# Dense layer in blocks of 512 and 256 tokens instead of 384, and the small steps of ranks and places moved between the slices of the first expert

## The chip, the cores and the metric

The kernel runs on one core of a Trainium2 chip. The core has a matrix engine (PE; its weight loads are listed as PEld), a vector engine (DVE), a scalar engine (ACT), GpSimd (POOL) and a sync engine (SP) that here only issues DMAs. Each engine works through its own instructions in program order and waits on semaphores for the others. The metric is the device time of one execution in microseconds (us), the median of several runs. Runs of this kernel spread over about 0.14%.

## The reference, cut to what matters

Three stages are computed one after another: windowed attention, a mixture of eight experts of which each token takes one, and a dense two-layer block.

```python
# attention: B=4, H=8, S=576, D=64, window 128  ->  x of 2304 tokens x 512
# experts: E=8, 512 -> 1024 -> 512
expert_idx = np.argmax(logits, axis=1)
gate_w = probs[np.arange(N), expert_idx]
for e in range(E):
    mask = expert_idx == e
    h = np.maximum(x[mask] @ w1[e], 0.0)
    out[mask] = gate_w[mask, None] * (h @ w2[e])
# dense layer: 512 -> 2048 -> 512, w_in and w_out are given as float64
h = x @ w_in
g = np.where(h >= 1, h, np.where(h <= -1, 0.0, (h + 1) ** 2 / 4))
return g @ w_out
```

## The kernel before

Attention and routing fill the first 180 us. Their order is chosen at build time by a small planner (`drive`), which places steps by assumed costs. After it the program is written out by hand in plain order.

**Experts.** Experts are taken by rank, that is, by how many tokens chose them. Each is done in eight slices `ff` of 128 hidden units. A slice has 12 matmuls into a PSUM tile `bh` (tokens x first weights, three products of high and low parts: `xh`, `xl`, `whi`, `wlo`), then ACT makes `hh` (L1463) and DVE makes `hl` (L1464, the low part), and 12 matmuls into `by` (L1447 to L1449) use `hh` and `hl` one slice later: PE runs the 12 of slice ff+1 before the second 12 of slice ff. Between slices stand, on ACT and DVE, the splitting of raw weights into `whi` (L555) and `wlo` (L560), from slice 2 the tokens of the next expert (`xh`, `xl`), and from expert 1 on a generator `side`: sorting of token numbers, then the conversion of dense weights.

**Ranks and places.** Before the first expert's first `hl`, DVE reorders the table of gates by rank (`by_rank(gtable, gtable)`, L328 and L330) and works out where each expert's tokens start (`starts`, L1172 to L1193). `erank_i` from it is read by SP for the loads of later experts' weights.

**Dense weights.** `conv64` turns float64 weights of one 128-unit chunk into high and low float32 parts: for each of the two matrices DVE runs L1059, L1061, L1064 and the low part (`wc_0l`, `wc_1l`, L1052), and ACT runs L1043 (`cvr`) and L1067 (the high part). `NEARLY = 5` chunks are converted among the experts, the other 11 in the dense layer, from its third `in_part` on.

**Dense layer.** The 2304 tokens lie in six blocks of 384. `RUNS` takes blocks 0 and 1 together, 2 and 3 together, then 4, then 5. For each of 16 chunks `ff` of a block, `in_part` has 12 matmuls (L1539 to L1541) into one of two PSUM tiles `ch`; then ACT (`r`, L1545), DVE (L1547, L1549, the last to read `ch`), ACT (`gh`, L1550) and DVE (`gl`, L1553) form the activation. `out_part` runs, one chunk later (two in the last runs), three matmuls (L1565 to L1567) for each 128 tokens into one of six PSUM tiles `o`. At a block's end `put` copies each tile out (ACT L1579, DVE L1581 by turns) and POOL scatters it to the output (L1584). The input of a block is loaded by `load_y` and split by `split_y` (L1133, L1134).

Of the kernel before, what the change touches and what calls it, by code (L numbers as in the profile page):

```python
# [20 lines left out]
P = 128  # L21
# [10 lines left out]
CAPS = (384, 376, 344, 314, 296, 286, 274, 256)  # L32
L2, L3 = 2, 4
NRAW, NW, LEAD = 6, 7, 5
NEARLY = 5
BIAS = {"V": 1.2}
CONV = ((0, 0.0, 0.0), (1, 0.9, 1.5), (2, 3.0, 3.0), (3, 4.5, 4.5))
PEN = (0.03, 0.0, 0.8)
# [7 lines left out]
KEY = 4096  # L46
EVAC_DVE = (1, 3, 5, 7)
CT = CAP // P
GT, HT = 768, 384
QF = S - S % P  # L50
NSLOT = E * CT
NQ = NP * NT
# [4 lines left out]
def f(ap):  # L57
    return ap.bitcast(F32)
# [3 lines left out]
def fused_kernel(ctx, tc, qk, vT, v, emb, tau, w1, w2, win64, wout64, out):  # L62
# [956 lines left out]
    permu = const.tile([P, NQ], U32, name="permu")  # L1019
    pce = pool(ctx, "pce", 1)  # L1020
    pcv = pool(ctx, "pcv", 1)
    py = pool(ctx, "py", 3)
    wch = {}

    raw64 = {}
# [93 lines left out]
                nc.vector.tensor_scalar(at, at, float(P), None, op0=ALU.add)  # L1119
                nc.vector.tensor_scalar(rel_, rel_, -float(P), None, op0=ALU.add)  # L1120

    yt = {}

    def load_y(i):
        yl = py.tile([P, 4, CAP], F32R, tag="xl", name="yl")
        yh = py.tile([P, 4, CAP], F32R, tag="xh", name="yh")
        nc.sync.dma_start(f(yl), ysT[:, i * HT:(i + 1) * HT].rearrange("(c p) s -> p c s", p=P))
        yt[i] = (yh, yl)

    def split_y(i):  # L1130
# [6 lines left out]
    with ExitStack() as bb:  # L1137
# [122 lines left out]
        def order():  # L1260
            yield ask({"G": 2.1}, after=["rows"] + of_tiles("out", 0, NQ))
            gather(0)
            seen["gathered"] = end[0] + 2.5
            yield ask({"V": 0.66}, after=["ranked"], late=LATE[4])
            with nc.allow_low_precision(reason="whole numbers, of which one is not zero"):
                by_rank(tabu, table)
            yield ask({"G": 3.2}, end[0] + 0.13)
            gather(1)
            yield ask({"V": 0.66}, after=[("gates", NP - 1)], late=LATE[4])
            by_rank(gtable, gtable)  # L1270

        def ranks_and_starts():
            yield vec(0.1, ["count"], late=LATE[4])
            for _ in rank_experts():
                yield vec(0.15, late=LATE[4])
            seen["ranked"] = end[0] + 0.13
            yield vec(0.15, late=LATE[4])
            for _ in starts():
                yield vec(0.15, late=LATE[4])

        def new_xT():
            xh = py.tile([P, 4, CAP], F32R, tag="xh", name="xh")
            xl = py.tile([P, 4, CAP], F32R, tag="xl", name="xl")
# [136 lines left out]
        for e in range(E):  # L1420
# [31 lines left out]
            for ff in range(8):  # L1452
# [59 lines left out]

    pcl = pool(ctx, "pcl", 1)
    pg = pool(ctx, "pg", 3)
    po = pool(ctx, "po", 2)
    ps_h = pool(ctx, "ps_ch", 2, space=PSUM)
    ps_o = pool(ctx, "ps_co", 1, space=PSUM)
    gap = const.tile([1, 1], F32, name="gap")
    halfc = const.tile([P, 1], F32, name="halfc")
    nc.gpsimd.memset(halfc, 0.5)  # L1520
    cv = conv64(range(NEARLY, FF // P), pcl)
    TH = HT // P

    RUNS = (((0, 1), 0, 1), ((2, 3), 0, 1), ((4,), 0, 2), ((5,), TH, 2))
    outs, parts = {}, [0]

    def more():

# [3 lines left out]
    def in_part(hf, ff):  # L1532
        parts[0] += 1
        w1h, w1l = wch[ff][:2]
        yh, yl = yt[hf]
        hp = ps_h.tile([P, HT], F32, tag="ch", name="ch")
        for c in range(4):
            o = slice(c * P, (c + 1) * P)
            nc.tensor.matmul(hp, w1h[:, o], yh[:, c], start=(c == 0), stop=False)  # L1539
            nc.tensor.matmul(hp, w1h[:, o], yl[:, c], start=False, stop=False)  # L1540
            nc.tensor.matmul(hp, w1l[:, o], yh[:, c], start=False, stop=(c == 3))  # L1541
        r = pg.tile([P, HT], F32, tag="r", name="r", bufs=2)
        a = pg.tile([P, HT], F32R, tag="gh", name="gh", bufs=4)
        b = pg.tile([P, HT], F32R, tag="gl", name="gl", bufs=4)
        nc.scalar.activation(r, hp, AF.Relu, bias=halfc, scale=0.5)  # L1545
        more()
        nc.vector.scalar_tensor_tensor(r, r, 1.0, r, op0=ALU.min, op1=ALU.mult)  # L1547
# [7 lines left out]
        return a, b  # L1555

    def out_tile(run, ff, gs, i, t):
        halves, b0, _ = run
        _, _, w2h, w2l = wch[ff]
        hf = halves[i]  # L1560
        gh, gl = gs[i]
        if ff == 0:
            outs[hf, t] = ps_o.tile([P, DM], F32, tag=f"o{b0 + i * TH + t}", name=f"o{b0 + i * TH + t}")
        o, out_ = slice(t * P, (t + 1) * P), outs[hf, t]
        nc.tensor.matmul(out_, gh[:, o], w2h, start=(ff == 0), stop=False)  # L1565
        nc.tensor.matmul(out_, gl[:, o], w2h, start=False, stop=False)  # L1566
        nc.tensor.matmul(out_, gh[:, o], w2l, start=False, stop=(ff == FF // P - 1))  # L1567
        if ff == FF // P - 1:
            put(hf, t)

    def out_part(run, ff, gs):
        for i in range(len(gs)):
            for t in range(TH):
                out_tile(run, ff, gs, i, t)

    def put(hf, t):
        ot = po.tile([P, DM], F32, tag="ot", name="ot", bufs=3)
        if t % 2 == 0:
            nc.scalar.activation(ot, outs.pop((hf, t)), AF.Copy)  # L1579
        else:  # L1580
            nc.vector.tensor_copy(ot, outs.pop((hf, t)))  # L1581
        k = hf * TH + t
# [5 lines left out]

    todo, coming = [], iter(())
    for run in RUNS:  # L1590
        halves, _, lag = run
        ahead = [h for h in (halves[0] + 2, halves[0] + 3) if len(halves) == 2 and h < N // HT]
        if ahead:
            load_y(ahead[0])
            coming = split_y(ahead[0])
        for ff in range(FF // P):
            gs = []
            for hf in halves:
                gs.append(in_part(hf, ff))
                if ahead and ff == FF // P - 1 and hf == halves[0]:  # L1600
                    del yt[hf]
                    load_y(ahead[1])
# [56 lines left out]
```

## Time and profile before

| | |
|---|---|
| time before, median of 3 runs | 822.54 us (822.37 to 823.5) |
| the profiled execution's own time | 822.19 us |
| its span, first to last instruction | 820.5 us |
| PE busy | 806.9 us (98%) |
| DVE busy | 516.9 us (63%) |
| ACT busy | 421.5 us (51%) |
| POOL busy | 137.7 us (17%) |
| mean DMA rate | 129 GB/s |
| granted TensorE clock, mean | 0.999 |

PE is busy nearly all the time, so the question for each stage is whether it ever waits, and how long one matmul takes from its start to the start of the next. The busy time of a matmul row overlaps the next one's, since matmuls are pipelined; distances between starts are what counts. The span is 1.69 us shorter than the execution's own time.

### The profile page before, as it was taken

To read this page: it belongs to the slowest core of one execution; us is meant where nothing else is said; L and a number is where in the kernel's file an instruction comes from. 1 tells how busy PE (TensorE), PEld (TensorE's weight loads), DVE (VectorE), ACT (ScalarE), POOL (GpSimd) and SP (SyncE) were. 2 spreads that over 40 slices of the span, in tenths; PEclk is the share of its full clock that TensorE was granted. 3 is DMA by queue.
4 is the path that set the end of the run, shared out by engine and by line. 5 is a ranking of instruction groups with operands and counts; after the bars stand their busy time and mean duration, and the time that the engine had idled before them with its cause. 6 is when DMAs were issued, how large, how long until landed. Compare 5 with 4: busy or idle time off the path is not lost.

```text
span 820.5 us, 14256 instructions
## 1 busy us (share of the span) xinstructions
PE 806.9 (98%) x5242; PEld 749.8 (91%) x5242; DVE 516.9 (63%) x1390; ACT 421.5 (51%) x881; POOL 137.7 (17%) x205
## 2 busy tenths in 40 slices
PE   9999999999999999999999999999999999999996
PEld 7999999869999999999998989999999999999995
DVE  7777767897667687777469898544343454344332
ACT  7879899856435466566345555333222333223221
POOL 5975664031110110100000000011000003001001
PEclk9999999999999999999999999999999999999999
DMA  9846942648645668776134332021000012001001
GB/s 335 308 158 237 330 160 71 227 160 277 202 159 166 216 216 276 241 235 198 62 116 128 129 122 84 1 100 55 0 1 1 1 40 77 1 1 40 1 0 39
DMA packets 59180, 106.03 MB, mean 129 GB/s; under 512 B 3942, under 2 KB 35686, under 8 KB 59104
## 3 DMA queue, kind: packets, MB, share of 16 engines
q1 hardware_dynamic: 55776, 95.15, 34.7%
q0 software_dynamic: 3328, 9.90, 3.5%
q8 instruction: 43, 0.70, 0.3%
q14 instruction: 33, 0.27, 0.1%
HBM read 90.42 MB, written 14.62 MB: 128 GB/s over the span
## 4 chain that ended last, share of the span: by engine, by line
issue 56%; PE 12%; POOL 2%; ACT 0%; DVE 0%; POOLq 0%; ACTq 0%
PE bh L1458 2%; POOL out L1584 2%; PE bh L1460 2%; PE bh L1459 2%; PE by L1447 2%; PE by L1449 2%; PE by L1448 2%; PE bx L1295 1%; ACT whi L555 0%; DVE wlo L560 0%; POOL gap L1583 0%; PE permp L1385 0%; POOLq L1655 0%; POOL xg L1166 0%; ACT yo L1497 0%
## 5 line engine op out<-in xcount | busy, mean ns | idle before, releaser
L1547 DVE SCALAR_TENSOR_TENSOR r<-r 128x384 f32<-128x384 f32 x96 | 53.4, 556 | 120.6 <-ACT r L1545 117.1
L1539 PE MATMUL ch<-yh,wc_0h 128*128 128x384 f32 x384 | 129.2, 336 | 0.0
L1541 PE MATMUL ch<-yh,wc_0l 128*128 128x384 f32 x384 | 129.1, 336 | 0.0
L1540 PE MATMUL ch<-yl,wc_0h 128*128 128x384 f32 x384 | 128.7, 335 | 0.0
L1545 ACT ACTIVATE r<-ch,halfc 128x384 f32<-128x384 f32 x96 | 55.2, 575 | 117.4 <-PE ch L1541 117.1
L1550 ACT ACTIVATE gh<-r 128x384 fp32r<-128x384 f32 x96 | 50.5, 526 | 123.4 <-DVE r L1549 123.4
L1566 PE MATMUL o<-wc_1h,gl 128*128 128x512 f32 x288 | 113.3, 393 | 0.1
L1567 PE MATMUL o<-wc_1l,gh 128*128 128x512 f32 x288 | 113.3, 393 | 0.0
L1565 PE MATMUL o<-wc_1h,gh 128*128 128x512 f32 x288 | 112.0, 389 | 0.0
L1584 POOL DMA_INDIRECT out<-ot,permu x18 | 17.5, 973 | 462.2 <-ACT ot L1579 458.9
L560 DVE TENSOR_TENSOR wlo<-wraw,whi 128x1024 fp32r<-128x1024 f32 x64 | 78.0, 1222 | 20.1 <-ACT whi L555 19.6
L1553 DVE TENSOR_TENSOR gl<-r,gh 128x384 fp32r<-128x384 f32 x96 | 53.4, 557 | 43.7 <-ACT gh L1550 42.6
L1458 PE MATMUL bh<-xh,whi 128*128 128x256 f32 (+6 forms) x256 | 80.2, 313 | 0.0
L1448 PE MATMUL by<-hl,whi 128*128 128x256 f32 (+6 forms) x256 | 77.5, 303 | 1.8 <-DVE hl L1464 1.8
L1447 PE MATMUL by<-hh,whi 128*128 128x256 f32 (+6 forms) x256 | 77.3, 302 | 0.0
L1449 PE MATMUL by<-hh,wlo 128*128 128x256 f32 (+6 forms) x256 | 77.3, 302 | 0.0
L1460 PE MATMUL bh<-xh,wlo 128*128 128x256 f32 (+6 forms) x256 | 77.1, 301 | 0.0
L1459 PE MATMUL bh<-xl,whi 128*128 128x256 f32 (+6 forms) x256 | 76.9, 301 | 0.0
L1539 PEld LDWEIGHTS ch<-yh,wc_0h 128*128 128x128 f32 x384 | 72.1, 188 | 2.9 <-DVE r L1549 0.3
L1540 PEld LDWEIGHTS ch<-yl,wc_0h 128*128 128x128 f32 x384 | 72.1, 188 | 2.5
L1541 PEld LDWEIGHTS ch<-yh,wc_0l 128*128 128x128 f32 x384 | 72.0, 188 | 0.0
L555 ACT ACTIVATE whi<-wraw 128x1024 fp32r<-128x1024 f32 x64 | 67.3, 1055 | 0.7 <-ACTq L1476 0.7
(270 smaller groups left out, 1718.9 us busy)
## 6 DMA issues: line engine op xcount, KB each, us to landing
wraw<-in_w SPq DMA_DIRECT2D x64, 512.0 KB, 4.6
rqk<-in_qk SPq DMA_DIRECT2D x30, 576.0 KB, 5.1
raw<-in_w_in SPq DMA_DIRECT2D x16, 512.0 KB
raw<-in_w_out SPq DMA_DIRECT2D x16, 512.0 KB, 4.7
vT<-in_vT SPq DMA_DIRECT2D x16, 288.0 KB, 2.8
yl<-ysT SPq DMA_DIRECT2D x6, 768.0 KB, 6.0
x_dram<-xt SPq DMA_DIRECT2D x8, 512.0 KB, 6.6
vt<-in_v SPq DMA_DIRECT2D x8, 438.0 KB, 6.8
```

What stands on the lines that cost most here:

```text
L1447: nc.tensor.matmul(y, w2h[:, o], hh[:, :cap], start=(ff == 0), stop=False)
L1448: nc.tensor.matmul(y, w2h[:, o], hl[:, :cap], start=False, stop=False)
L1449: nc.tensor.matmul(y, w2l[:, o], hh[:, :cap], start=False, stop=(ff == 7))
L1458: nc.tensor.matmul(hp, w1h[:, o], xh[:, c, :cap], start=(c == 0), stop=False)
L1459: nc.tensor.matmul(hp, w1h[:, o], xl[:, c, :cap], start=False, stop=False)
L1460: nc.tensor.matmul(hp, w1l[:, o], xh[:, c, :cap], start=False, stop=(c == 3))
L1539: nc.tensor.matmul(hp, w1h[:, o], yh[:, c], start=(c == 0), stop=False)
L1540: nc.tensor.matmul(hp, w1h[:, o], yl[:, c], start=False, stop=False)
L1541: nc.tensor.matmul(hp, w1l[:, o], yh[:, c], start=False, stop=(c == 3))
L1565: nc.tensor.matmul(out_, gh[:, o], w2h, start=(ff == 0), stop=False)
L1566: nc.tensor.matmul(out_, gl[:, o], w2h, start=False, stop=False)
L1567: nc.tensor.matmul(out_, gh[:, o], w2l, start=False, stop=(ff == FF // P - 1))
```

## The change

- **Blocks.** The dense layer's tokens lie in blocks of 512, 256, 512, 512 and 512 (`SIZES`). The first run takes the blocks of 512 and 256 together, the others one block each. `in_part` writes a `ch` tile of up to 512 columns, two of them as before. Output tiles take the six PSUM tiles `o` in turn.
- **Buffers.** Expert tokens (`xh`, `xl`) move to a pool of two buffers of their own; the dense blocks have places of their own (`yl0`, `yl1`, `yl2`). `gh` and `gl` have two buffers of each width; those of the last block lie in the space of the fourth block's input, four deep. Output copies use the conversion's `cvr` and `cva` buffers, two each, in place of three `ot`.
- **Early chunks.** `NEARLY` goes from 5 to 3, so 13 chunks are converted in the dense layer.
- **Ranks and places.** Of `starts`, only the part up to `erank_i` stays ahead of the first expert. The rest, with the gate table put by rank, is called two steps at a time after each slice of expert 0 from slice 1 on.

```diff
-NEARLY = 5
+NEARLY = 3
...
-GT, HT = 768, 384
+SIZES = (512, 256, 512, 512, 512)
+GT = max(SIZES)
...
-    py = pool(ctx, "py", 3)
+    py = pool(ctx, "py", 1)
...
     def load_y(i):
-        yl = py.tile([P, 4, CAP], F32R, tag="xl", name="yl")
-        yh = py.tile([P, 4, CAP], F32R, tag="xh", name="yh")
-        nc.sync.dma_start(f(yl), ysT[:, i * HT:(i + 1) * HT].rearrange("(c p) s -> p c s", p=P))
+        t0, n = sum(SIZES[:i]), SIZES[i]
+
+        place, tag = ((py, 0), (py, 1), (late[0], 2), (py, 0), (late[0], 2))[i]
+        yl = place.tile([P, 4, n], F32R, tag=f"yl{tag}", name="yl")
+        yh = place.tile([P, 4, n], F32R, tag=f"yh{tag}", name="yh")
+        nc.sync.dma_start(f(yl), ysT[:, t0:t0 + n].rearrange("(c p) s -> p c s", p=P))
...
             nc.vector.tensor_copy(erank_i, erank)
             yield
+            by_rank(gtable, gtable)
+            yield
             pick(nc.vector, nov, cnt, True, tmp)
...
-            yield ask({"V": 0.66}, after=[("gates", NP - 1)], late=LATE[4])
-            by_rank(gtable, gtable)
...
-            yield vec(0.15, late=LATE[4])
-            for _ in starts():
-                yield vec(0.15, late=LATE[4])
...
         drive(lambda: streams)
+        places = starts()
+        next(places)
...
                 if e > 0:
                     for _ in range(3 if e < 3 else 2):
                         next(side, None)
+                elif ff > 0:
+
+                    for _ in range(2):
+                        next(places, None)
...
-    RUNS = (((0, 1), 0, 1), ((2, 3), 0, 1), ((4,), 0, 2), ((5,), TH, 2))
-    outs, parts = {}, [0]
+    RUNS = ((0, 1), (2,), (3,), (4,))
+    first_tile = [sum(SIZES[:i]) // P for i in range(len(SIZES))]
+    outs, parts, wide = {}, [0], []
...
-        hp = ps_h.tile([P, HT], F32, tag="ch", name="ch")
+        n = SIZES[hf]
+        hp = ps_h.tile([P, GT], F32, tag="ch", name="ch")[:, :n]
...
-        a = pg.tile([P, HT], F32R, tag="gh", name="gh", bufs=4)
-        b = pg.tile([P, HT], F32R, tag="gl", name="gl", bufs=4)
+        r = pg.tile([P, GT], F32, tag="r", name="r", bufs=2)[:, :n]
+        if hf == len(SIZES) - 1:
+
+            if ff == 0:
+                wide.extend(py.tile([P, 4, GT], F32R, tag=f"{t}0", name=f"{t}w") for t in ("yh", "yl"))
+            a, b = (w[:, ff % 4] for w in wide)
+        else:
+            a = pg.tile([P, n], F32R, tag=f"gh{n}", name="gh", bufs=2)
+            b = pg.tile([P, n], F32R, tag=f"gl{n}", name="gl", bufs=2)
...
+            bank = (first_tile[hf] + t) % 6
+            outs[hf, t] = ps_o.tile([P, DM], F32, tag=f"o{bank}", name=f"o{bank}")
...
-        ot = po.tile([P, DM], F32, tag="ot", name="ot", bufs=3)
+
+        ot = f(pcv.tile([P, 512], I32, tag=("cvr", "cva")[t % 2], name="ot", bufs=2))
...
-        halves, _, lag = run
-        ahead = [h for h in (halves[0] + 2, halves[0] + 3) if len(halves) == 2 and h < N // HT]
-        if ahead:
-            load_y(ahead[0])
-            coming = split_y(ahead[0])
+        halves, lag = run, 2 if run == RUNS[-1] else 1
+        if halves[-1] + 1 < len(SIZES):
+            load_y(halves[-1] + 1)
+            coming = split_y(halves[-1] + 1)
...
-    for n, t in ((0, 0), (1, 0), (0, 1), (1, 1), (0, 2), (1, 2)):
-        out_tile(*todo[n], 0, t)
+
+    for t in range(SIZES[-1] // P):
+        for step in todo:
+            out_tile(*step, 0, t)
```

Three places show how instructions move; all are on DVE. The line numbers of the changed kernel are larger than those of the kernel before by 2 to 15 for the same statement.

The first place is the start of expert 0. In the kernel before, the 20 steps of ranks and places stand between the last `xl` (low part of the tokens of expert 0) and the first `hl`; these are the last ten of them and what follows:

```order
L1181 CAST sti<-stf 128x8
L1182 TENSOR_TENSOR nov<-nov,caps 128x8
L1184 TENSOR_SCALAR nov<-nov 128x8
L1185 CAST novi<-nov 128x8
L1187 TENSOR_SCALAR novi<-novi 128x8
L1188 TENSOR_REDUCE anyo<-novi 128x1
L149 TENSOR_TENSOR tmp_2996<-rank1h,stf 128x64
L150 TENSOR_REDUCE ste<-tmp_2996 128x8
L1192 SCALAR_TENSOR_TENSOR kbase<-erank,caps 128x8
L1193 TENSOR_SCALAR toki<-tokhi,pid 128x18
L1464 SCALAR_TENSOR_TENSOR hl<-bh,hh 128x256
L560 TENSOR_TENSOR wlo<-wraw,whi 128x1024 x2
```

In the changed kernel, from that last `xl` on:

```order
L1292 TENSOR_TENSOR xl<-bx,xh 128x256 x4
L1177 MEMSET one_2986 128x8
L151 TENSOR_TENSOR tmp_2996<-rank1h,ranks 128x64
L152 TENSOR_REDUCE erank<-tmp_2996 128x8
L1179 CAST erank_i<-erank 128x8
L1468 SCALAR_TENSOR_TENSOR hl<-bh,hh 128x256
L562 TENSOR_TENSOR wlo<-wraw,whi 128x1024 x2
L1468 SCALAR_TENSOR_TENSOR hl<-bh,hh 128x256
L562 TENSOR_TENSOR wlo<-wraw,whi 128x1024
L330 TENSOR_TENSOR tm<-gtable,rank1h 128x192
L332 TENSOR_REDUCE gtable<-tm 128x24
L151 TENSOR_TENSOR tmp_2996<-rank1h,cnt 128x64
```

Four of the 20 steps are left ahead of the first `hl`; the other 16 stand in groups of four behind the slices 1 to 4.

The second place is the start of expert 6 (`hl` of 274 columns). Before, behind the copies `yo` of the last expert's result and a `wlo`, steps of the conversion (`cva`, `wc_1l`) stand ahead of the second and third `hl`:

```order
L560 TENSOR_TENSOR wlo<-wraw,whi 128x1024
L1061 SCALAR_TENSOR_TENSOR cva<-raw_7005,cva 128x512
L1064 ISA cva<-cva,cvr 128x1024
L1464 SCALAR_TENSOR_TENSOR hl<-bh,hh 128x274
L560 TENSOR_TENSOR wlo<-wraw,whi 128x1024
L1070 TENSOR_TENSOR wc_1l<-cva,wc_1h 128x512
L1464 SCALAR_TENSOR_TENSOR hl<-bh,hh 128x274
L560 TENSOR_TENSOR wlo<-wraw,whi 128x1024
L1134 TENSOR_TENSOR yl<-yl,yh 128x384
```

In the changed kernel:

```order
L562 TENSOR_TENSOR wlo<-wraw,whi 128x1024
L1468 SCALAR_TENSOR_TENSOR hl<-bh,hh 128x274
L562 TENSOR_TENSOR wlo<-wraw,whi 128x1024
L1468 SCALAR_TENSOR_TENSOR hl<-bh,hh 128x274
L562 TENSOR_TENSOR wlo<-wraw,whi 128x1024
L1139 TENSOR_TENSOR yl<-yl,yh 128x512
L1468 SCALAR_TENSOR_TENSOR hl<-bh,hh 128x274
```

The conversion steps are gone from here; they belong to the fifth chunk, which the change leaves to the dense layer.

The third place is the start of the dense layer, `r` and `gl` being the two results of the activation on DVE. Before:

```order
L1547 SCALAR_TENSOR_TENSOR r<-r 128x384
L1549 TENSOR_TENSOR r<-ch,r 128x384
L1553 TENSOR_TENSOR gl<-r,gh 128x384
L1547 SCALAR_TENSOR_TENSOR r<-r 128x384
L1549 TENSOR_TENSOR r<-ch,r 128x384
L1553 TENSOR_TENSOR gl<-r,gh 128x384
L1547 SCALAR_TENSOR_TENSOR r<-r 128x384
L1059 TENSOR_SCALAR cva<-raw_7108 128x512
```

In the changed kernel:

```order
L1562 SCALAR_TENSOR_TENSOR r<-r 128x512
L1564 TENSOR_TENSOR r<-ch,r 128x512
L1568 TENSOR_TENSOR gl<-r,gh 128x512
L1562 SCALAR_TENSOR_TENSOR r<-r 128x256
L1564 TENSOR_TENSOR r<-ch,r 128x256
L1568 TENSOR_TENSOR gl<-r,gh 128x256
L1562 SCALAR_TENSOR_TENSOR r<-r 128x512
L1061 TENSOR_SCALAR cva<-raw_6629 128x512
```

The passes are the same in number and order; the first `in_part` has passes of 512 columns and the second of 256, where both had 384.

## Rows read from the trace of the kernel before

**Rows 1.** PE by stage: window, length, busy (count), clock, DMA share, GB/s.

```profile
181.85:413.82 231.97, 229.33 (x1659) 1.00 0.62 200
413.82:684.01 270.19, 270.19 (x1370) 1.00 0.18 59
684.01:814.07 130.06, 129.98 (x649) 1.00 0.05 19
```

**Rows 2.** Waits of PE's weight loads over the whole span; total us, times, longest.

```profile
PEld by L1448 <- DVE hl L1464: 2.5, 3, 1.7
...
PEld o L1566 <- DVE gl L1553: 0.4, 1, 0.4
...
PEld ch L1539 <- DVE r L1549: 0.3, 2, 0.2
```

**Rows 3.** Timeline of PE, expert 0; columns: start, length, instruction, idle before.

```profile
185.55 0.28 PE L1447 MATMUL by<-hh,whi 128*128 128x256 f32 x1
187.37 0.39 PE L1448 MATMUL by<-hl,whi 128*128 128x256 f32 x1 [1.54 <-DVE hl L1464]
```

**Rows 4.** Timeline of ACT (first row) and DVE, expert 0.

```profile
183.95 0.38 ACT L1463 ACTIVATE hh<-bh 128x256 fp32r<-128x256 f32 x1 [0.89 <-PE bh L1460]
...
183.06 0.41 DVE L328 TENSOR_TENSOR tm<-gtable,rank1h 128x192 f32<-128x192 f32 x1
...
186.76 0.23 DVE L1193 TENSOR_SCALAR toki<-tokhi,pid 128x18 f32<-128x18 f32 x1
186.90 0.41 DVE L1464 SCALAR_TENSOR_TENSOR hl<-bh,hh 128x256 fp32r<-128x256 f32 x1
```

**Rows 5.** Timeline of PE (two rows) and DVE, start of expert 6.

```profile
370.90 0.29 PE L1447 MATMUL by<-hh,whi 128*128 128x274 f32 x1
...
371.65 0.29 PE L1449 MATMUL by<-hh,wlo 128*128 128x274 f32 x1
...
369.60 0.68 DVE L1061 SCALAR_TENSOR_TENSOR cva<-raw,cva 128x512 int32<-128x512 int32 x1
...
370.93 0.43 DVE L1464 SCALAR_TENSOR_TENSOR hl<-bh,hh 128x274 fp32r<-128x274 f32 x1
```

**Rows 6.** Timeline of PE: first matmuls of stretches, expert 0 and first dense run.

```profile
190.22 0.28 PE L1447 MATMUL by<-hh,whi 128*128 128x256 f32 x1
...
191.66 0.28 PE L1458 MATMUL bh<-xh,whi 128*128 128x256 f32 x1
...
447.30 0.39 PE L1565 MATMUL o<-wc_1h,gh 128*128 128x512 f32 x1
...
451.42 0.33 PE L1539 MATMUL ch<-yh,wc_0h 128*128 128x384 f32 x1
...
455.61 0.39 PE L1565 MATMUL o<-wc_1h,gh 128*128 128x512 f32 x1
```

**Rows 7.** Timelines at the start of the dense layer: ACT, DVE, PE.

```profile
416.16 0.58 ACT L1545 ACTIVATE r<-ch,halfc 128x384 f32<-128x384 f32 x1 [2.12 <-PE ch L1541]
...
417.37 0.56 DVE L1549 TENSOR_TENSOR r<-ch,r 128x384 f32<-128x384 f32 x1
...
417.98 0.44 PE L1539 MATMUL ch<-yh,wc_0h 128*128 128x384 f32 x1
```

**Rows 8.** Groups by line (three from 510 us): busy, mean ns, idle.

```profile
L1549 DVE TENSOR_TENSOR r<-ch,r 128x384 f32<-128x384 f32 x72 | 40.1, 557 | 2.5
...
L1579 ACT ACTIVATE ot<-o 128x512 f32<-128x512 f32 x12 | 6.8, 592 | 12.7 <-DMA out<-ot,permu 9.2 <-PE o L1567 3.6
L1581 DVE COPY ot<-o 128x512 f32<-128x512 f32 x6 | 4.1, 687 | 9.7 <-DMA out<-ot,permu 7.5 <-PE o L1567 2.2
...
L560 DVE TENSOR_TENSOR wlo<-wraw,whi 128x1024 fp32r<-128x1024 f32 x64 | 78.0, 1222 | 20.1 <-ACT whi L555 19.6
```

**Rows 9.** Timeline of ACT, two places of the first dense run.

```profile
445.48 0.58 ACT L1545 ACTIVATE r<-ch,halfc 128x384 f32<-128x384 f32 x1 [0.35 <-PE ch L1541]
...
469.25 0.67 ACT L1043 ACTIVATE cvr<-raw 128x512 int32<-128x512 uint32 x1 [0.63 <-DMA raw<-in_w_in]
```

More of the change, by code (lines that the diff above doesn't have):

```diff
@@ L1120, in overflow @@
                 nc.vector.tensor_scalar(rel_, rel_, -float(P), None, op0=ALU.add)
-    yt = {}
+    yt, late = {}, [None]
     def load_y(i):
-        yl = py.tile([P, 4, CAP], F32R, tag="xl", name="yl")
-        yh = py.tile([P, 4, CAP], F32R, tag="xh", name="yh")
-        nc.sync.dma_start(f(yl), ysT[:, i * HT:(i + 1) * HT].rearrange("(c p) s -> p c s", p=P))
+        t0, n = sum(SIZES[:i]), SIZES[i]
[3 more added lines that the diff above has]
+        nc.sync.dma_start(f(yl), ysT[:, t0:t0 + n].rearrange("(c p) s -> p c s", p=P))
         yt[i] = (yh, yl)
@@ L1276, in ranks_and_starts @@
             seen["ranked"] = end[0] + 0.13
-            yield vec(0.15, late=LATE[4])
-            for _ in starts():
-                yield vec(0.15, late=LATE[4])
         def new_xT():
-            xh = py.tile([P, 4, CAP], F32R, tag="xh", name="xh")
-            xl = py.tile([P, 4, CAP], F32R, tag="xl", name="xl")
+            xh = px.tile([P, 4, CAP], F32R, tag="xh", name="xh")
+            xl = px.tile([P, 4, CAP], F32R, tag="xl", name="xl")
             return xh, xl
@@ L1514, in fused_kernel @@
     pg = pool(ctx, "pg", 3)
-    po = pool(ctx, "po", 2)
+    late[0] = pool(ctx, "pz", 1)
     ps_h = pool(ctx, "ps_ch", 2, space=PSUM)
@@ L1521, in fused_kernel @@
     cv = conv64(range(NEARLY, FF // P), pcl)
-    TH = HT // P
-    RUNS = (((0, 1), 0, 1), ((2, 3), 0, 1), ((4,), 0, 2), ((5,), TH, 2))
-    outs, parts = {}, [0]
+    RUNS = ((0, 1), (2,), (3,), (4,))
+    first_tile = [sum(SIZES[:i]) // P for i in range(len(SIZES))]
+    outs, parts, wide = {}, [0], []
     def more():
@@ L1541, in in_part @@
             nc.tensor.matmul(hp, w1l[:, o], yh[:, c], start=False, stop=(c == 3))
-        r = pg.tile([P, HT], F32, tag="r", name="r", bufs=2)
-        a = pg.tile([P, HT], F32R, tag="gh", name="gh", bufs=4)
-        b = pg.tile([P, HT], F32R, tag="gl", name="gl", bufs=4)
+        r = pg.tile([P, GT], F32, tag="r", name="r", bufs=2)[:, :n]
[6 more added lines that the diff above has]
+            b = pg.tile([P, n], F32R, tag=f"gl{n}", name="gl", bufs=2)
         nc.scalar.activation(r, hp, AF.Relu, bias=halfc, scale=0.5)
@@ L1557, in out_tile @@
     def out_tile(run, ff, gs, i, t):
-        halves, b0, _ = run
+        halves = run
         _, _, w2h, w2l = wch[ff]
@@ L1562, in out_tile @@
         if ff == 0:
-            outs[hf, t] = ps_o.tile([P, DM], F32, tag=f"o{b0 + i * TH + t}", name=f"o{b0 + i * TH + t}")
+            bank = (first_tile[hf] + t) % 6
+            outs[hf, t] = ps_o.tile([P, DM], F32, tag=f"o{bank}", name=f"o{bank}")
         o, out_ = slice(t * P, (t + 1) * P), outs[hf, t]
@@ L1572, in out_part @@
         for i in range(len(gs)):
-            for t in range(TH):
+            for t in range(SIZES[run[i]] // P):
                 out_tile(run, ff, gs, i, t)
     def put(hf, t):
-        ot = po.tile([P, DM], F32, tag="ot", name="ot", bufs=3)
+        ot = f(pcv.tile([P, 512], I32, tag=("cvr", "cva")[t % 2], name="ot", bufs=2))
         if t % 2 == 0:
@@ L1581, in put @@
             nc.vector.tensor_copy(ot, outs.pop((hf, t)))
-        k = hf * TH + t
+        k = first_tile[hf] + t
         nc.gpsimd.memset(gap, 0.0)
@@ L1599, in fused_kernel @@
                 gs.append(in_part(hf, ff))
-                if ahead and ff == FF // P - 1 and hf == halves[0]:
-                    del yt[hf]
-                    load_y(ahead[1])
             todo.append((run, ff, gs))
@@ L1607, in fused_kernel @@
                 next(coming, None)
-        if ahead:
-            for _ in split_y(ahead[1]):
-                pass
-    for n, t in ((0, 0), (1, 0), (0, 1), (1, 1), (0, 2), (1, 2)):
-        out_tile(*todo[n], 0, t)
+    for t in range(SIZES[-1] // P):
+        for step in todo:
+            out_tile(*step, 0, t)
 _OUTS = [((2304, 512), "float32")]
```

## Prediction

> **What bounds the kernel now.** I read the stages first. From the first expert to the dense layer PE is busy 229.33 of 231.97 us, in the first two runs of the dense layer all of 270.19, in the last two 129.98 of 130.06, always at the granted clock 1.00, which is the upper of its two levels, 2.4 GHz [rows 1]. So from 181.85 us on the time is the number of matmuls times the distance between their starts, plus the few waits. Then the waits of PE's weight loads [rows 2]: the reader is to see that three lines matter to this change. The second product of a slice waits for `hl` three times, 2.5 us in all and 1.7 at the longest; the dense layer waits 0.3 us for the last reader of a `ch` tile, in two places, and 0.4 us once at its end for `gl`. DVE and ACT cost nothing where they are not in these lines. Third, the timeline at each of these places [rows 3 to 5, 7], and last, the starts of long stretches of matmuls, which give their true price [rows 6]: the row's own length overlaps the next.
>
> **The change part by part.** *Ranks and places.* In expert 0 PE starts the first matmul into `by` at 185.55 and the second at 187.37, 1.82 us later where 0.12 is usual [rows 3, 6]. It waits for `hl`, which DVE starts at 186.90. Its input `hh` was done at 183.95 + 0.38 = 184.33; but DVE worked from 183.06 on through the 20 small steps, the last at 186.76 [rows 4]. With four steps left ahead of it (the order of the changed kernel), the small steps end near 183.8, `hl` waits for `hh` and is done near 184.8, 0.9 before PE asks. That takes off 1.82 - 0.12 = 1.7 us. The other 16 steps are not free, they are about 0.2 us each, 0.8 behind each of slices 1 to 4. A slice of PE is 24 matmuls of 0.12, or 2.9 us; DVE's own work in it is one `wlo` of 1.22 [rows 8], one `hl` of 0.41 [rows 4] and, from slice 3, an `xl` of about 0.5: with 0.8 more, 2.5 to 2.9. Since `hl` is asked for a whole stretch of 12 matmuls after PE made its input (1.4 us), I take no new wait. Bounds of this term: 1.7 off, or, if a later `hl` comes as late as 1.2 us of one `wlo`, 0.5 off. Behind the moved steps wait the gate scaling of expert 1 on ACT (in slice 2, after the gate table, which comes in slice 1) and the store of expert 0 (in expert 1); neither is near. `erank_i`, for which SP waits before it loads the ninth raw weight, comes a little earlier.
>
> *Three early chunks instead of five.* In expert 6, two conversion steps stand ahead of `hl` on DVE: it starts L1061 at 369.60 and `hl` only at 370.93, and PE takes 0.75 us from 370.90 to 371.65 for two matmuls [rows 5]. The other short wait for `hl` is of the same kind. Both belong to chunks that the change leaves to the dense layer. What is left of the line is 2.5 - 1.7 = 0.8 us [rows 2], and I take all of it off. The cover is checked at the other end: the dense layer converts one chunk in each pair of `in_part`, as before, so a chunk is ready about a pair (8.3 us) ahead of its use rather than three; the rate is the same.
>
> *Blocks.* Run 1 before: 18 matmuls of 512 columns take 451.42 - 447.30 = 4.12 us, 0.2289 each; 24 of 384 take 455.61 - 451.42 = 4.19, 0.1746 each; 12 of 256, in expert 0, take 191.66 - 190.22 = 1.44, 0.120 each [rows 6]. Columns stay (2304 x 16 x 12), second-layer matmuls stay (18 tiles x 16 x 3 = 864). First-layer ones go from 6 x 16 x 12 = 1152 of 384 to 4 x 16 x 12 = 768 of 512 and 192 of 256: 1152 x 0.1746 = 201.1 us become 768 x 0.2289 + 192 x 0.120 = 198.8, so 2.3 off. The three prices lie on a line with about 11 ns per matmul whatever its columns, and 192 matmuls are saved. Bounds: nothing, if the price of a 512-column first-layer matmul is that of 384 by columns (0.2328), and 2.9, if all 15 ns beyond the columns at 2.4 GHz (0.2289 against 0.2133) belong to the matmul.
>
> The Trainium skill (TensorE: Matmul & The Clock Gate, section Back-to-back issue gap) gives an isolated gap of N / 2.4 + 2.5 ns, that is 2.5 ns per matmul where these rows show some 11. By it the blocks would save 192 x 2.5 ns = 0.5 us.
>
> *The first wait of the dense layer.* PE does the first chunk of both blocks and then wants the first `ch` tile back. Before, 24 matmuls x 0.1746 = 4.2 us after its start at 413.82 it had just been read: ACT starts at 416.16, DVE's last pass at 417.37 ends at 417.93, PE goes on at 417.98 [rows 7]. Now the same 4.2 us pass (12 x 0.2289 + 12 x 0.120), but the first block's 12 matmuls end later by 12 x 0.054 = 0.65, and its passes are longer: DVE 0.687 in place of 0.557 twice, a copy standing for the two, and ACT about 0.1 longer (0.58 at 384 [rows 7]; at 512 between 0.592, a plain copy, and 0.58 x 512 / 384 = 0.77) [rows 8]. The tile was free 417.93 - 413.82 = 4.11 after the start, and is now at 4.11 + 0.65 + 0.26 + 0.10 = 5.1: PE waits 0.9 to 1.0 instead of 0.2, 0.8 more (0.7 to 0.95). The second tile, of 256, is free in time.
>
> *The rest.* At the end, the last `gl` is later by three DVE passes and two of ACT, but out matmuls of four tiles rather than three cover it: 0.4 stays. The last copy is DVE's (0.687) instead of ACT's (0.592) [rows 8]: 0.1 more. Loads of inputs go out earlier than they are needed, into free places; more output buffers can only shorten waits that PE does not see. I take nothing for these.
>
> **Sum:** -1.7 - 0.8 - 2.3 + 0.8 + 0.1 = -3.9 us. The profiled execution takes 822.19, its span 820.5; the median of the runs is 822.54, 0.35 above. So span 816.6, own time 818.3, median 818.6.
>
> **The rivals.** *Price by column.* A larger matmul saves nothing, because what lies beyond the columns grows with them: 512 columns at 0.2328. For it: no row has a first-layer matmul of 512. Against it: 256, 384 and 512 lie on one line that does not pass through zero [rows 6]. Then 818.6 + 2.3 = 820.9. With the 2.5 ns per matmul of the Trainium skill (same page and section) it would be 820.4; the rows do not agree with that constant.
>
> *The stall in expert 0 moves.* The small steps meet `wlo` and `xl` in slices 2 to 4 where DVE is full; one late `hl` gives back up to 1.2: 819.8. Against it: 1.4 us of notice.
>
> *The converter chain of run 1 becomes the bound, and the kernel is slower.* ACT and DVE in turn serve the activation and a chunk's conversion; in a pair of `in_part` (8.3 us) ACT has only 0.35 us in which it waits for PE, so the chain takes 7.95 [rows 9]. Now 13 pairs convert instead of 11, the splits of the next input (four DVE passes of 0.687) fall on three pairs that also convert, and in a 512 part the raw load has less time between its issue and its use; one load already made ACT wait 0.63 [rows 9]. If every pair overruns by x, 13 x is lost, once the slack before PE misses the second `ch` tile (about 2 us, an estimate: half a pair, less the passes) has been used up by the three splits, 3 x 0.687 = 2.1. With the 0.63 wait in every pair, x = 0.63 - 0.35 = 0.28: 3.6 lost, 822.2, no change. It is slower by 0.2% (1.65 us) from x = (3.9 + 1.65) / 13 = 0.43 on; with two such waits per pair, x = 0.91, it gives 830.4. Against it: only two loads of the run show a wait at all, and DVE's columns per pair are the same (768).
>
> **How the numbers follow.** 0.2% is about what a measurement of this kernel can tell from no change. My forecast, 817.3 to 819.6 by the bounds of its terms, 0.62; price by column 0.13; moved stall 0.08; converter chain 0.11, of which 0.04 near 822 and 0.07 slower; any other loss or gain 0.06. Faster than 820.9: the forecast, the moved stall, half of price by column (0.06, since it ends on the line) and 0.02 of the rest, so 0.78; slower: 0.07 of the chain and 0.01 of the rest, so 0.08; within 0.2%: what is left, 0.14. The range 816.6 to 821.4 holds the forecast, the first two rivals and a margin for a larger saving; what is left out is the chain and half of the rest.
>
> **What the next profile shows.** Right: no wait of PE for `hl` in expert 0, 5 or 6; the dense layer starts near 411.3; 12 matmuls of 512 into `ch` in about 2.75 us and a pair of run 1 still near 8.3, a chunk of a single block at 5.5; one wait of about 1 us for the first `ch` tile. Wrong: a wait for `ch` repeated through run 1 (chain), a 512 matmul at 0.233 (price by column), a wait for `hl` in slices 2 to 4 of expert 0.

## Result and the profile after

The changed kernel takes 814.07 us (median of 4 runs, 813.93 to 814.38), the one before, measured beside it, 822.64. The ratio is 0.9892, interval 0.988 to 0.9904: 8.6 us less, where I had forecast 3.9 less and 816.6 as the lower end. The direction and the places were right; the size was not. The profiled execution takes 813.93 us, its span is 812.2, 8.3 shorter than before.

First the stages of the profile after (for the same statement its line numbers are 2 to 17 larger than before, not 2 to 15): experts, the first run of the dense layer, its other three runs. The columns are window, length, busy time and count of PE, PEld, DVE, ACT and POOL, then clock, DMA share and GB/s; they answer to [rows 1].

```profile
181.86:410.36 228.50, 227.93 (x1658) 223.35 (x1657) 153.60 (x295) 123.19 (x210) 20.16 (x21) 1.00 0.60 194
410.36:539.63 129.27, 128.41 (x656) 109.71 (x655) 110.19 (x205) 66.39 (x120) 0.00 (x0) 1.00 0.37 118
539.63:805.47 265.84, 265.60 (x1170) 219.25 (x1169) 109.27 (x160) 72.08 (x113) 17.06 (x33) 1.00 0.05 19
```

The experts take 228.50 us instead of 231.97, so 3.47 less (I had 2.5). From the first matmul of the dense layer to the start of its last are 805.47 - 410.36 = 395.11, before 813.84 - 413.82 = 400.02, so 4.91 less (I had 1.5). The granted clock is 1.00 as before, so none of it comes from the clock. What lies behind is the same to 0.1 us.

The waits of PE's weight loads after (total us, times, longest) answer to [rows 2]:

```profile
PEld ch L1548 <- DVE r L1564: 1.1, 1, 1.1
...
PEld o L1582 <- DVE gl L1568: 0.5, 1, 0.5
...
PEld o L1582 <- DVE ylw L1568: 0.5, 1, 0.5
```

No line for `hl` is left. The wait for the last reader of a `ch` tile is there once, 1.1 us. The second line, 0.5 us, is new and is looked at below; the third is the wait at the end of [rows 2], with `gl` now called `ylw`.

Expert 0 on PE and the start of the dense layer, in the timeline of PE after (start, length, instruction, idle before); they answer to [rows 3] and [rows 7]:

```profile
185.56 0.28 PE L1451 MATMUL by<-hh,whi 128*128 128x256 f32 x1
185.68 0.28 PE L1452 MATMUL by<-hl,whi 128*128 128x256 f32 x1
...
414.42 0.28 PE L1550 MATMUL ch<-yh,wc_0l 128*128 128x256 f32 x1
415.56 0.50 PE L1548 MATMUL ch<-yh,wc_0h 128*128 128x512 f32 x1 [0.86 <-DVE r L1564]
...
555.17 0.50 PE L1582 MATMUL o<-wc_1h,gl 128*128 128x512 f32 x1 [0.19 <-DVE gl L1568]
...
642.12 0.39 PE L1581 MATMUL o<-wc_1h,gh 128*128 128x512 f32 x1
...
644.84 0.39 PE L1548 MATMUL ch<-yh,wc_0h 128*128 128x512 f32 x1
...
647.56 0.39 PE L1581 MATMUL o<-wc_1h,gh 128*128 128x512 f32 x1
```

In expert 0 the second matmul into `by` follows 0.12 us after the first, not 1.82. At 415.56 is the wait for the first `ch` tile. The last three rows are where the unexpected gain lies: a stretch (matmuls one behind the other into one kind of tile) of twelve matmuls of 512 columns takes 2.72 us, 0.2267 each, whether it writes `o` or `ch`, and each of the twelve takes the same. The row from which I took my price, 0.2289, was the mean of a stretch before [rows 6], and its matmuls do not all take the same. The timeline of PE before, in the third run:

```profile
686.12 0.39 PE L1565 MATMUL o<-wc_1h,gh 128*128 128x512 f32 x1
...
688.20 0.33 PE L1539 MATMUL ch<-yh,wc_0h 128*128 128x384 f32 x1
...
688.72 0.35 PE L1539 MATMUL ch<-yh,wc_0h 128*128 128x384 f32 x1
688.91 0.34 PE L1540 MATMUL ch<-yl,wc_0h 128*128 128x384 f32 x1
...
689.26 0.33 PE L1539 MATMUL ch<-yh,wc_0h 128*128 128x384 f32 x1
...
690.30 0.39 PE L1565 MATMUL o<-wc_1h,gh 128*128 128x512 f32 x1
```

Nine matmuls of 512 take 688.20 - 686.12 = 2.08 us, where 9 x 0.2267 is 2.04; twelve of 384 take 690.30 - 688.20 = 2.10 (2.106 as a mean over 30 such stretches). The last six of the twelve, from 689.26 on, lie 0.1733 apart, which would make 2.08; from the fourth to the fifth are 0.19. In the stretches of 18, the first nine lose the same 0.04 and the other nine lie at 0.2267. So before the change each pair of stretches lost 0.041 + 0.026 = 0.067 us near its start, with no wait in any row. There are some 62 pairs: 4.1 us.

Two things could do that. (Each run below has its own Theory A and Rival B, in the text put on record before it; these two are what the runs on width are about.) **Theory A:** PE loses time when the width of its matmuls changes, 384 to 512 and back; in the changed kernel the single blocks have 512 in both layers. **Theory B:** the passes of ACT and DVE over `ch`, which begin when a stretch into `ch` ends and last about as long as the first nine matmuls into `o`, slow PE.

### The profile page after: what moved, and what is told of

It reads as the page before. It is cut to its first block, busy times and chain, and to the rows that moved or that the text cites. A ratio compares the mean times of both kernels' runs of the same rounds, so it can differ in the third digit from the quotient of the medians.

```text
span 812.2 us, 13749 instructions
## 1 busy us (share of the span) xinstructions
PE 799.3 (98%) x5050; PEld 715.1 (88%) x5050; DVE 512.3 (63%) x1341; ACT 414.7 (51%) x842; POOL 138.6 (17%) x205
## 4 chain that ended last, share of the span: by engine, by line
PE 59%; issue 10%; DVE 2%; ACT 1%; POOL 1%; POOLq 0%; DVEq 0%; ACTq 0%
PE ch L1548 6%; PE ch L1550 6%; PE ch L1549 6%; PE o L1582 6%; PE o L1581 6%; PE o L1583 6%; PE bh L1462 4%; PE by L1451 4%; PE by L1453 4%; PE by L1452 4%; PE bh L1464 3%; PE bh L1463 3%; PE bx L1297 1%; POOL out L1601 1%; DVE r L1564 0%
## 5 line engine op out<-in xcount | busy, mean ns | idle before, releaser
L1562 DVE SCALAR_TENSOR_TENSOR r<-r 128x512 f32<-128x512 f32 x80 | 51.0, 637 | 118.7 <-ACT r L1560 116.9
L1548 PE MATMUL ch<-yh,wc_0h 128*128 128x512 f32 (+1 forms) x320 | 117.8, 368 | 0.9 <-DVE r L1564 0.9
L1549 PE MATMUL ch<-yl,wc_0h 128*128 128x512 f32 (+1 forms) x320 | 117.7, 368 | 0.0
L1550 PE MATMUL ch<-yh,wc_0l 128*128 128x512 f32 (+1 forms) x320 | 117.7, 368 | 0.0
L1560 ACT ACTIVATE r<-ch,halfc 128x512 f32<-128x512 f32 x80 | 51.3, 641 | 119.1 <-PE ch L1550 118.4
L1582 PE MATMUL o<-wc_1h,gl 128*128 128x512 f32 x224 | 87.4, 390 | 0.2 <-DVE gl L1568 0.2
L1581 PE MATMUL o<-wc_1h,gh 128*128 128x512 f32 x224 | 87.3, 390 | 0.0
L1583 PE MATMUL o<-wc_1l,gh 128*128 128x512 f32 x224 | 87.1, 389 | 0.0
L1565 ACT ACTIVATE gh<-r 128x512 fp32r<-128x512 f32 x64 | 37.1, 579 | 97.7 <-DVE r L1564 96.3
L1467 ACT ACTIVATE hh<-bh 128x256 fp32r<-128x256 f32 (+6 forms) x64 | 27.0, 421 | 83.7 <-PE bh L1464 82.0
```

## Experiments

**Which part brings what.** The kernel before with the early chunks alone, and with the places too; then the changed kernel with the old places.

```diff
-NEARLY = 5
+NEARLY = 3
```

> The kernel before with only three early chunks instead of five. Theory A: the waits of experts 5 and 6 for conversion steps go (0.85 us in expert 5, 0.6 in expert 6, some 0.2 in small pieces), time 822.5 - 1.7 = 820.8. My prediction's term was 0.8, which would give 821.7. Rival B (the conversions cost in the dense layer what they save in the experts): 822.5.

Measured: 821.33 us, ratio 0.9981 (0.9972 to 0.999). The interval, 0.8 to 2.3 us less, cannot tell the 0.8 of my prediction from the 1.7 of this run's Theory A; the stage can. In its profile the experts stage is 230.51 us, 1.46 less than before, and the dense layer 400.03, unchanged with 13 conversions in place of 11.

```diff
-NEARLY = 5
+NEARLY = 3
...
+            by_rank(gtable, gtable)
+            yield
...
-            yield ask({"V": 0.66}, after=[("gates", NP - 1)], late=LATE[4])
-            by_rank(gtable, gtable)
...
-            yield vec(0.15, late=LATE[4])
-            for _ in starts():
-                yield vec(0.15, late=LATE[4])
...
+        places = starts()
+        next(places)
...
+                elif ff > 0:
+                    for _ in range(2):
+                        next(places, None)
```

> The kernel before with only the moved ranks and places and with three early chunks instead of five; the blocks stay at 384. Theory A (the gain of the experts stage is its own, 1.8 us from the late hl of expert 0 and 1.7 us from the conversion steps of two chunks, which delayed not only hl but also the copies that the transposes of tokens wait for): the dense layer begins near 410.4 us and keeps its 400.0 us, time 822.5 - 3.5 = 819.1. Rival B (part of the gain of that stage hangs on the blocks, by the earlier or smaller loads of the dense layer's inputs, and the 13 conversions in the dense layer cost something): time 820 to 821.

Measured: 819.18 us, ratio 0.9961 (0.9948 to 0.9975). Stage of experts 228.71, 3.26 less than before and 1.80 less than with the early chunks alone; dense layer 400.03. This run's Theory A holds: the two parts act in the experts stage alone, and they add up. The changed kernel showed 3.47, 0.2 more; five other runs here with the same code in that stage have 228.7 to 228.8 us for it, so 0.2 is what one execution differs from another.

The next one puts back, in the changed kernel, the lines on places that the second diff shows, with `NEARLY = 3` and the blocks kept.

```diff
-            by_rank(gtable, gtable)
-            yield
...
+            for _ in starts():
+                yield vec(0.15, late=LATE[4])
...
-                elif ff > 0:
-                    for _ in range(2):
-                        next(places, None)
```

> The changed kernel with the ranks and places put back ahead of expert 0. Theory A (the terms of the experts stage and of the blocks add up): PE waits again for the hl of expert 0, 1.8 us, and all else stays: 814.07 + 1.8 = 815.9. Rival B (in the changed kernel the moved steps delay something else in slices 1 to 4, or a later slack takes the 1.8 us back): 814.1 to 815.3.

Measured: 816.26 us, ratio to the kernel before 0.9917 (0.9904 to 0.9931), so about 2 us above the changed kernel. Its experts stage is 230.30, 1.80 longer, and PE waits 1.8 us for `hl`, once. Theory A of this run holds too; nothing takes the 1.8 us back later.

**Width or activation.** Two kernels that change only the width of the second layer's matmuls, each in one of the two kernels, so that the passes of ACT and DVE stay as they are. Both leave out the other 128 columns in chunks 1 to 14.

```diff
-        nc.tensor.matmul(out_, gh[:, o], w2h, start=(ff == 0), stop=False)
+        m = DM if ff in (0, FF // P - 1) else 384
+        y = out_[:, :m]
+        nc.tensor.matmul(y, gh[:, o], w2h[:, :m], start=(ff == 0), stop=False)
...
```

> The kernel before; in chunks 1 to 14 the second layer's matmuls take only the first 384 of 512 columns, so these columns of the output lack the sum of those chunks. All matmuls of the dense layer but those of chunks 0 and 15 are then 384 wide, and ACT and DVE do the same passes as before. Theory A (PE loses 0.04 us at the start of each stretch into the output and 0.025 us early in each stretch into ch because the width changes between 384 and 512): in the last two runs the twelve matmuls into ch take 12 x 0.1735 = 2.08 us with no slow ones at places 3 to 6 and the nine into the output 9 x 0.1735 = 1.56 us. Rival B (the passes of the activation, which run beside the first nine matmuls into the output, slow PE): 2.11 and 1.60, with slow matmuls at the same places as before. The time falls by about 756 x 0.053 = 40 us, if the activation does not become the bound.

> The changed kernel; in chunks 1 to 14 the second layer's matmuls take only the first 384 of 512 columns, so these columns of the output lack the sum of those chunks. In the single blocks of 512 the width now changes twice in a pair of stretches, where in the changed kernel it did not change. Theory A (the change of width costs): slow matmuls appear at places 3 to 6 of a stretch or in its first nine, 0.02 to 0.04 us for each stretch: 2.74 to 2.76 us for twelve into ch (2.72 without), 2.10 to 2.12 for twelve of 384 into the output (2.08 without). Rival B (the activation's passes): nothing new beside the present distances, 2.72 and 2.08.

The first took 785.25 us, the second 787.35 (one run each). In the first run of blocks of either, PE now waits for the activation, so the single blocks are read. The timeline of PE in the kernel before with 384 columns in both layers:

```profile
667.71 0.33 PE L1567 MATMUL o<-wc_1h,gh 128*128 128x384 f32 x1
...
669.27 0.33 PE L1539 MATMUL ch<-yh,wc_0h 128*128 128x384 f32 x1
...
669.79 0.33 PE L1539 MATMUL ch<-yh,wc_0h 128*128 128x384 f32 x1
669.96 0.33 PE L1540 MATMUL ch<-yl,wc_0h 128*128 128x384 f32 x1
...
671.35 0.33 PE L1567 MATMUL o<-wc_1h,gh 128*128 128x384 f32 x1
```

Nine into `o` take 1.56 us and twelve into `ch` 2.08, 0.1733 each; from the fourth to the fifth are 0.17. The loss is gone, with the same passes of the activation beside it. In the same execution chunks 0 and 15, which keep 512 columns, still have it: 2.081 us for nine and 2.106 for twelve. And in the changed kernel with 512 into `ch` and 384 into `o`:

```profile
642.64 0.39 PE L1548 MATMUL ch<-yh,wc_0h 128*128 128x512 f32 x1
...
645.40 0.33 PE L1583 MATMUL o<-wc_1h,gh 128*128 128x384 f32 x1
...
645.93 0.35 PE L1583 MATMUL o<-wc_1h,gh 128*128 128x384 f32 x1
646.11 0.34 PE L1584 MATMUL o<-wc_1h,gl 128*128 128x384 f32 x1
...
647.51 0.39 PE L1548 MATMUL ch<-yh,wc_0h 128*128 128x512 f32 x1
```

Twelve of 512 now take 2.76 us (2.761 as a mean over the 40 stretches of the last three runs that follow one of 384; 2.72 in the changed kernel), twelve of 384 take 2.106. The pair loses 0.041 + 0.026 = 0.067 us: the numbers of before, though the layers have changed places and `o` is now the one with 384. Theory A holds and B falls: the loss goes with the width, not with the layer or the activation.

**Twice the changes, nothing else.** The kernel before, with the output stretch of the first block drawn between the two stretches into `ch`. Every matmul, pass and load stays.

```diff
-            gs = []
-            for hf in halves:
+            gs, prev = [], todo[0] if len(halves) == 2 and todo and todo[0][0] is run else None
+            for i, hf in enumerate(halves):
                 gs.append(in_part(hf, ff))
+                if prev:
+                    for t in range(TH):
+                        out_tile(*prev, i, t)
```

> The kernel before; in the first two runs, the nine matmuls into the output that belong to the first block come between the two stretches into ch, where both blocks' stretches into ch came first. Nothing is added; the width changes four times in a pair of in_part where it changed twice, in about 30 pairs. Theory A (a change from 384 to 512 and back costs 0.065 us): 30 x 0.065 = 2.0 us more, 824.5, if no wait of another kind comes or goes. Rival B (the cost belongs to the activation after a pair of blocks, or is no more than a way of recording it): 822.5.

Measured: 824.87 us, ratio 1.0022 (1.0013 to 1.0031). Its dense layer takes 401.90, 1.88 more than before: 30 more pairs of stretches at 0.067 are 2.0, and the first wait of the dense layer costs 0.13 less. The timeline of PE in the first two runs:

```profile
502.15 0.33 PE L1539 MATMUL ch<-yh,wc_0h 128*128 128x384 f32 x1
...
504.26 0.39 PE L1565 MATMUL o<-wc_1h,gh 128*128 128x512 f32 x1
...
506.34 0.33 PE L1539 MATMUL ch<-yh,wc_0h 128*128 128x384 f32 x1
```

2.11 and 2.08 us; the means over 89 stretches of each kind are 2.106 and 2.081, those of before. The loss is in the time, not only in the rows.

**The price of one matmul more.** The changed kernel with each 512-column matmul into `o` made as two of 256.

```diff
+        full = ff in (0, FF // P - 1)
+        for m in (slice(0, 512),) if full else (slice(0, 256), slice(256, 512)):
+            nc.tensor.matmul(out_[:, m], gh[:, o], w2h[:, m], start=(ff == 0), stop=False)
...
```

> The changed kernel; in chunks 1 to 14 each matmul of the second layer with 512 columns is made as two of 256, with the same products and sums. 18 x 3 x 14 = 756 more matmuls, no more columns. Theory A (13.4 ns per matmul beyond its columns at 2.4 GHz, whatever the width, and a cost where the width changes, now twice in a pair of stretches of the last three runs): +756 x 13.4 ns = 10.1 us and up to 3 us for the changes, 824 to 827. Rival B (price by column): 814 to 817. With the 2.5 ns per matmul of the Trainium skill (TensorE: Matmul & The Clock Gate, Back-to-back issue gap) it would be 816 to 819.

Measured: 824.57 us (one run). The dense layer takes 405.33, 10.22 more than in the changed kernel, for 756 matmuls: 13.5 ns each, with what the changes of width add and two shorter waits take off. Price by column is out. In streams without a change of width, 512, 384 and 256 columns lie 226.7, 173.3 and 120 ns apart. That is one line: 0.417 ns for each column, and 13.3 ns for the matmul. The Trainium skill (TensorE: Matmul & The Clock Gate, Back-to-back issue gap) gives N / 2.4 + 2.5 ns for an isolated matmul; as an estimate, 756 more of them would by it have added 1.9 us. The measured 10.2 us do not agree with it.

**What the loss depends on.** The same edit as for 384, with 448 and with 320; the columns beyond are left out in chunks 1 to 14 again.

```diff
-        m = DM if ff in (0, FF // P - 1) else 384
+        m = DM if ff in (0, FF // P - 1) else 448
```

> The changed kernel; in chunks 1 to 14 the second layer's matmuls take the first 448 of 512 columns, so the other columns of the output lack the sum of those chunks. Asked is what the loss at a change of width depends on: 512 and 384 lose 0.065 us in a pair of stretches, 512 and 256 only 0.02. Theory A (the loss is some constant of a change of width, and 256 is the exception): 0.06 to 0.07 in a pair of stretches of the single blocks, 12 x 0.2267 + 12 x 0.200 + 0.065 = 5.19 us. Rival B (the loss grows with the difference of the widths up to some point): 0.03 or less, 5.15.

> The changed kernel with the first 320 of 512 columns in the same matmuls; the other columns of the output lack the sum of those chunks. Theory A: 12 x 0.2267 + 12 x 0.1467 + 0.065 = 4.55 us for a pair of stretches of the single blocks. Rival B (as with 256, the loss falls as the narrower matmul gets narrower): 0.02 to 0.05, 4.50 to 4.53.

They took 800.51 and 772.59 us (one run each). In the single blocks, twelve of 512 beside twelve of 448 take 2.734 + 2.432 = 5.166 us, 0.046 above 12 x 0.2267 + 12 x 0.200; beside 320 they take 2.745 + 1.755 = 4.500, 0.020 above 12 x 0.2267 + 12 x 0.1467. With 384 it was 0.067. In the kernel with 256 the stretch of 512 takes 2.747, 0.027 more, and the 24 of 256 take 2.873, 0.007 less: 0.020. The prices 0.200 and 0.1467 are read off the line above; no run has 448 or 320 alone. For 448 that matters: its matmuls lie 0.199 to 0.208 apart, by the means of the places, to the end of the stretch and never settle at 0.200, so 0.032 of the 0.046 may be its price and no loss. What is sure is the loss in the stretch of 512: 0.014 beside 448, 0.041 beside 384, 0.025 beside 320, 0.027 beside 256. A constant loss (Theory A of these runs) is out. Their Rival B has its number at 320, and at 448 it hangs on the open price; a loss that rises or falls steadily with the narrower width does not fit all four. 384 beside 512, which is what the kernel before had, is the worst of the four.

A change of width is not the only thing that brings the slow places. In the changed kernel they also follow the wait at 555.17, where all widths are 512. The timeline of PE:

```profile
555.51 0.39 PE L1583 MATMUL o<-wc_1l,gh 128*128 128x512 f32 x1
...
557.12 0.39 PE L1581 MATMUL o<-wc_1h,gh 128*128 128x512 f32 x1
```

These seven distances make 1.616 us, one by one 0.231, 0.231, 0.236, 0.228, 0.233, 0.231 and 0.226, where 7 x 0.2267 is 1.587; then it is 0.2267 again. What a wait and a change of width have in common for PE, no run here shows.

**The first wait of the dense layer.** The changed kernel, with a third tile for `ch` lent by the output tile `o5`.

```diff
+        if parts[0] == 3:
+            hp = ps_o.tile([P, GT], F32, tag="o5", name="ch")[:, :n]
+        else:
-        hp = ps_h.tile([P, GT], F32, tag="ch", name="ch")[:, :n]
+            hp = ps_h.tile([P, GT], F32, tag="ch", name="ch")[:, :n]
```

> The changed kernel; the third call of in_part, the one that waits for the first ch tile, uses the bank of the output tile o5 instead, which is first written some 9 us later. Theory A (the stall at the start of the dense layer is this wait alone, 1.0 us): no wait for r in the dense layer's first 10 us, 814.07 - 1.0 = 813.05. Rival B (the activation of the first chunk is late for the first output tile too, so that the wait goes there, to gl or to o5): 814.1.

Measured: 812.93 us, ratio 0.988 (0.9865 to 0.9895), the fastest version here that does the whole work; the interval overlaps that of the changed kernel, 814.07 and 0.9892. The timeline of PE, at the same place:

```profile
414.78 0.28 PE L1553 MATMUL ch<-yh,wc_0l 128*128 128x256 f32 x1
414.90 0.40 PE L1551 MATMUL ch<-yh,wc_0h 128*128 128x512 f32 x1
```

0.12 us between the blocks, no wait, and none at the first output tile either, so the stall was this wait alone. The dense layer takes 393.47, 1.64 less than in the changed kernel: 1.17 for this wait with the slow matmuls behind it, and 0.49 for the one at 555.17 above, which does not come in this execution; its edit does not touch that place.

## Why the prediction fell short, step by step

**Ranks and places (1.7 off): right.** The first slice of expert 0 is 1.79 us shorter, and undoing the part costs 1.80. On DVE, in the timeline after, the place has four small steps and then `hl`, which waits for ACT and starts at 184.37, 1.3 us before PE wants it ([rows 4] had 186.90):

```profile
183.59 0.35 DVE L1179 CAST erank_i<-erank 128x8 int32<-128x8 f32 x1
184.37 0.42 DVE L1468 SCALAR_TENSOR_TENSOR hl<-bh,hh 128x256 fp32r<-128x256 f32 x1 [0.43 <-ACT hh L1467]
185.32 2.36 DVE L562 TENSOR_TENSOR wlo<-wraw,whi 128x1024 fp32r<-128x1024 f32 x2 [0.52 <-ACT whi L557]
```

The rival that the stall moves fell: no later `hl` is waited for.

**Three early chunks (0.8 off): the mechanism was right, the term too small.** The step that failed is "What is left of the line is 2.5 - 1.7 = 0.8 us [rows 2], and I take all of it off": I read one line of the waits. The conversion steps also delay, on ACT, the gate scaling of the next expert's tokens (`xg`), which PE's transposes into `bx` need, and that wait has a line of its own. The waits, and the timelines of ACT and PE in expert 5, before:

```profile
PEld bx L1295 <- ACT xg L1344: 0.5, 1, 0.5
```

```profile
344.81 0.63 ACT L1067 ACTIVATE wc_0h<-cva 128x512 fp32r<-128x512 f32 x1 [2.65 <-DVE cva L1064]
345.34 0.39 ACT L1463 ACTIVATE hh<-bh 128x286 fp32r<-128x286 f32 x1
345.63 1.05 ACT L555 ACTIVATE whi<-wraw 128x1024 fp32r<-128x1024 f32 x1
346.58 1.93 ACT L1344 ACTIVATE xg<-xg,gtable 128x512 f32<-128x512 f32 x3
```

```profile
347.86 0.44 PE L1295 MATMUL bx<-ident,xg 128*128 128x128 f32 x2
348.56 0.23 PE L1295 MATMUL bx<-ident,xg 18*128 18x18 f32 x1 [0.27 <-ACT xg L1344]
```

ACT stood 2.65 us waiting for DVE's conversion, then had to catch up on `hh`, `whi` and `xg`. In the changed kernel this slice is 0.54 us shorter, the two slices with a late `hl` 0.31 and 0.50, others some 0.3 together: 1.6 in all; 1.46 with this edit alone.

**Blocks (2.3 off): this step failed, it was 6.35.** Two sentences of it were wrong. The price: "18 matmuls of 512 columns take 451.42 - 447.30 = 4.12 us, 0.2289 each" is a mean that holds the loss at a change of width, and I put it on a kernel in which most widths no longer change; without the loss it is 0.2267, and 384 is 0.1733. And "second-layer matmuls stay": their number does, their time does not, since a part of it came from their neighbours. With the prices free of the loss, a matmul costs 13.3 ns beyond its columns where I had 11, and 192 fewer matmuls save 2.56 us. The changes of width took 4.11 us before; what is left is the first run, where 15 stretches of 18 into `o` take 4.108 instead of 18 x 0.2267 = 4.08, and those of 256 take 1.432 instead of 1.44: 0.32. So 3.79 come from there, a term that my sum did not have. Together 6.35, less 0.94 and 0.49 for the two waits below: 4.92, where the rows show 4.91. The line through three prices that made it look safe was drawn through means that held the loss too, 2.2 ns a matmul at 512 columns and 1.1 at 384. My bounds for this step did not come out of their own terms either: with 0.2328 at 512 and 0.120 kept at 256 the blocks would have cost 0.7 us, not nothing.

**The first wait of the dense layer (0.8 more): right.** PE goes on 5.20 us after its start at 410.36 (I had 5.1) and stands 1.03 us there against 0.2 before. Its first matmuls after a wait are slower too, here 0.34, 0.24 and 0.23 us apart; with them the loss is 1.19 against 0.25, so 0.94 more, inside my 0.7 to 0.95. With another tile it is gone.

**The rest (0): one step failed.** "More output buffers can only shorten waits that PE does not see." At the end of the first run a copy into an output buffer waits on ACT for the scatter of an earlier one, and the next block's `r` is behind it. The timeline of ACT after:

```profile
551.10 0.60 ACT L1596 ACTIVATE ot<-o 128x512 f32<-128x512 f32 x1 [4.71 <-DMA out<-ot,permu]
551.59 0.69 ACT L1560 ACTIVATE r<-ch,halfc 128x512 f32<-128x512 f32 x1
```

Its `gl` is late at 555.17, 0.58 us after the matmul before it, and with the slow matmuls behind the wait PE loses 0.49 us. How much it loses goes with the scatter: ACT stands 4.71 us here, 4.25 in the run with the old places and 4.19 in that with the third tile, and PE loses 0.49, 0.05 and nothing. Before, the same queue stood behind the scatter too, but the next block's stretch was 24 matmuls long there. That this length was the cover is argued, not tried. At the end of the program the wait for the last `gl` stayed, 0.37 us lost in both kernels, as I had said.

**The rivals.** Price by column fell. So did the converter chain as the bound: the first run has one wait for `ch` in its rows, and a pair with a conversion in it takes 8.26 us, its matmuls alone; with 13 conversions and the old blocks the dense layer takes the same 400.03. The forecast's own band, 817.3 to 819.6, is not what its bounds add up to, which is 817.9 to 822.3; the measured 814.07 lies below either, for the term of 3.79 that neither held.

## What to carry to other kernels

Before a mean distance between matmuls is used as a price, lay the stretches over one another and look at the distances by place: a loss without a wait shows only there, and it belongs to the neighbours, not to the matmul. Where the widths of a kernel's stretches can be made equal at the same number of columns, count the changes as well as the matmuls. And when work is taken off an engine, read every line of the waits for that engine, not only the line that led there.

## What the runs showed of the hardware

A change between matmuls of 384 and 512 columns cost PE 0.041 us in the stretch of 512 and 0.026 in the stretch of 384, spread over the first six to nine matmuls, with the granted clock at 1.00 and no wait in the rows. That is 0.067 for a pair, whichever layer has which width; it was 0.020 with 512 and 256, and, with the narrower price read off a line, 0.020 with 320 and up to 0.046 with 448. Slow matmuls of the same kind follow a wait where all widths are 512. Without either, 512, 384 and 256 columns lay 226.7, 173.3 and 120 ns apart. Why the loss is largest at 384, and what in PE loses the time, stays open.
